# Key-value products of a linear-attention kernel: whole-array products over blocks of 128 successive tokens in place of products on quarters of the array

## Chip, cores and metric

The kernel runs on one core of a Trainium2 chip. The time is the device time of one execution in microseconds (us), median over the timed runs. Engines are named as in the profile: PE is TensorE's matmuls, PEld its weight loads, DVE VectorE, ACT ScalarE, POOL GpSimd, SP SyncE, which issues nearly all DMAs.

## What is computed

A Performer attention block is followed by a Fourier mixing block with an MLP. All tensors are f32; there are 8 batches, 8 heads, 576 tokens and 64 channels a head, and 128 random features.

```python
def phi(x):
    proj = np.einsum('bhsd,md->bhsm', x, omega)
    ...
    return np.exp(h) / np.sqrt(m)
q_p, k_p = (phi(q_s), phi(k_s))
kv = np.einsum('bhsm,bhsd->bhmd', k_p, v)
z = np.sum(k_p, axis=2)
num = np.einsum('bhsm,bhmd->bhsd', q_p, kv)
den = np.einsum('bhsm,bhm->bhs', q_p, z)[..., None] + 1e-06
return (num / den).astype(np.float32)
```

The result, with the heads side by side as 512 channels, is Fourier-transformed over tokens and channels; the real part is added to it, the sum is normalised, and an MLP with weights of 512 x 2048 and 2048 x 512 is added. The change concerns `kv` and `z` alone: a sum over the 576 tokens of a head, and so indifferent to the order in which they are taken.

## The kernel before

**Pairs.** The attention works on 32 pairs of heads, 4 to a batch. `loads` (L464) brings the keys of a pair into the first nine 64-channel columns of the tile `kq` and its queries into the next nine; there are two `kq` buffers. `load_v` (L476) brings the values into one of three tiles `vd`, whose 65th column holds ones, so that the product gives `kv` and `z` at once. All three use the same arrangement: partition `p` of 128 holds nine successive tokens, partitions 0 to 63 those of the first head and 64 to 127 those of the second.

**Steps of a pair** (`attn`, L668). Nine transposes of 128 x 128 (L607) turn `kq`; the scores (L701) multiply the turned tokens with `omega`, on half rows of the array for the first six pairs (`wide`) and on quarters for the others; `softmax` (L637) takes the maximum on DVE (L644) and the exponential on ACT (L661). The features of chunk `c` are then a 128 x 128 tile with tokens on the partitions. The key-value products (L732 to L741) take a 64 x 64 quarter of a feature tile as weights, 64 tokens of one head by half of its 128 features, and stream the 65 columns of `vd`. Nine chunks by two heads by two halves make 36 products in a pair, accumulated in PSUM as `kvp[feature, head, column]`, each head in a bank of its own. The step's copy to SBUF (L749 on DVE, L751 on ACT) follows. Query features are transposed (L607 again), and the numerators (L782, L790) use `kv` and are scaled into the token tile (L799 to L811).

**Beside it.** In the same stretch of time run the Fourier products of finished batches (L894, L904, L944, L955), the narrowing of the MLP weights (L532 to L550, loaded by SP at L564) and the first MLP products (L1236, L1259). The rest of the span is the MLP (L1727, L1878, L2178).

**Order.** Everything is cut into `Step`s, each with its engine, its cost as planned and its dependences. `Listing.run` (L272) orders them from written-down choices, one character a step (`PICKS`) and one a PSUM bank (`BANKS`). The choices fix the order of instructions on every engine; planned costs don't change it where a choice is written. An engine runs its instructions in that order and waits where a tile isn't there.

Of the kernel before, what the change touches and what calls it, by code (L numbers as in the profile page):

```python
# [375 lines left out]
def kernel(  # L376
# [10 lines left out]
    nc = tc.nc  # L387

    B, H, S, D = q.shape
# [13 lines left out]
    P = 128  # L403

    R = S // 64

    NS = 3
    NV = 3
# [38 lines left out]
        kq=NKQ, turned=NS, e=NE, e1=NS, kv=NS, x0=1, x1=1, fold=1, half=1, y=1,  # L447
# [8 lines left out]
    def got():  # L456

        return listing.got, psum_of(listing.got)
# [2 lines left out]
    kqs = {}  # L461
    vds = []

    def loads():  # L464
        for n in range(B * NP):
            b, pr = divmod(n, NP)
            h = slice(2 * pr, 2 * pr + 2)
            rows = "i (p r) d -> (i p) r d"
            yield Step(SP, 0.37, 3.0, take=("kq",), makes=("k", n), kb=288)
            kq = ld.tile([P, 2 * R, D], F32, name="kq", tag="kq")  # L470
            nc.sync.dma_start(kq[:, 0:R, :], k[b, h].rearrange(rows, r=R))
            kqs[n] = kq
            yield Step(SP, 0.47, 3.6, makes=("kq", n), kb=288, bias=-2.98)
            nc.sync.dma_start(kq[:, R : 2 * R, :], q[b, h].rearrange(rows, r=R))

    def load_v(n):  # L476
        b, pr = divmod(n, NP)
        yield Step(SP, 0.63, 4.0, take=(f"vd{n % NV}",), makes=("vd", n), kb=500, bias=0.52)
        nc.sync.dma_start(
            vds[n % NV][:, :, 0:D],  # L480
            v[b, 2 * pr : 2 * pr + 2].rearrange("i (p r) d -> (i p) r d", r=R),
        )

    def loads_v():
        for n in range(B * NP):
            yield from load_v(n)
# [181 lines left out]
    def attn(n):  # L668
        b, pr = divmod(n, NP)

        yield Step(NONE, after=(("k", n),) + ((("vd", n - 1),) if n else ()))
        kq = kqs.pop(n)
# [40 lines left out]
        def place(c):  # L713
            if c in (R - 1, R):
                return 2, c - (R - 1)
            return (c % 2, c // 2) if c < R else (3 + c % 2, (c - R - 1) // 2)

        def feature(c):
            t, i = place(c)
            return es[t][:, i, :]  # L720
# [8 lines left out]
            give=("e", "e", f"vd{n % NV}"), bias=-0.19,  # L729
        )  # L730
        kvb, kvp = got()
        for r in range(R):  # L732
            for i, h in ((0, 0), (1, 1), (0, 1), (1, 0)):
                rows, cols = slice(D * i, D * i + D), slice(D * h, D * h + D)
                nc.tensor.matmul(  # L735
                    kvp[cols, i, 0 : D + 1],
                    lhsT=feature(r)[rows, cols],
                    rhs=vds[n % NV][rows, r, :],
                    start=(r == 0),
                    stop=(r == R - 1),  # L740
                )  # L741
        kvs = []

        def keep():
# [32 lines left out]
        for i in range(2):  # L777
            for c in range(4):
                half = int(c in (1, 2))
                for g in range(2):  # L780
# [3 lines left out]
                        lhsT=flat[:, c0 : c0 + D],  # L784
                        rhs=kvs[0][:, i, :],
                    )

        for i in range(2):
            for g in range(2):
                nc.tensor.matmul(  # L790
                    ndp[D * g : D * g + D, i, (D + 1) * 4 : (D + 1) * 5],
                    lhsT=qeT[:, 0, D * i : D * i + D],
                    rhs=kvs[0][:, i, :],
# [775 lines left out]
    def pairs(start):  # L1569
        for n in range(start, B * NP, NS):  # L1570
            yield from attn(n)
# [45 lines left out]
    def betweens(text):  # L1617
# [6 lines left out]
    listing = Listing(buffers)  # L1624
    listing.run(
        [first(), loads(), loads_v(), load_tables(), frames(), plain_norms(), mixing()]
        + [pairs(i) for i in range(NS)]
        + [w2_parts(), weight_sums(), block_norms(0, mlpp), plain(), weights(), warm()],
# [766 lines left out]
```

## Time and profile before

| | |
|---|---|
| timed runs | 1120.97 us median of 3 (1120.73 to 1124.49) |
| profiled execution, span from first to last instruction | 1119.2 us |
| TensorE clock granted | 0.999 of full speed, on average |
| DMA | 196549 packets, 236.13 MB, 53808 of them under 512 B |
| DVE's maxima (L644) | 89.3 us in all |
| ACT's exponentials (L661) | 165.7 us in all |

The profile has no time of the profiled execution other than its span. A row of a group of instructions has its line, engine and operation, the tiles written and read, the part of the array (`64*64` is a quarter, `128*128` the whole), the size, the count, then busy time in us and the mean of one in ns. An f32 product is recorded as two passes, a transpose as one. Passes of different parts of the array may overlap, and the recorded duration of one holds a fixed tail, so distances between starts say more than durations. A row of the timeline has start, length, engine, line and count; instructions of one kind that follow each other are merged into one row. A row of the chain has start, length and what was being done.

### The profile page before, as it was taken

What the parts mean: (1) busy time and instruction counts of PE and PEld (TensorE: products, weight loads), DVE (VectorE), ACT (ScalarE), POOL (GpSimd) and SP (SyncE); (2) the same over time, 40 slices, a digit from 0 to 9 for tenths busy, and PEclk for the clock granted to TensorE, in tenths of its full rate; (3) what the DMA queues carried; (4) which work ended last, traced back from release to release, by engine and by line L of the source; (5) the groups of instructions that cost most, each with busy time, mean ns of one, the idle gap of its engine ahead of it and who ended that gap; (6) DMA issues with size and microseconds to landing.
All of it is one profiled execution on the core that took longest, in us unless ns stands there. A gap on an engine that the chain in (4) does not pass through costs nothing.

```text
span 1119.2 us, 31666 instructions
## 1 busy us (share of the span) xinstructions
PE 1108.4 (99%) x12467; PEld 1000.4 (89%) x12467; DVE 888.7 (79%) x1685; ACT 539.5 (48%) x1644; POOL 390.6 (35%) x401
## 2 busy tenths in 40 slices
PE   9999999999999999999999999999999999999998
PEld 7888888879868778999999889999889999889998
DVE  6999999987576767687697777888677888568895
ACT  7998898856536455623214452223463223331221
POOL 2443443553563348634413464000365000152000
PEclk9999999999999999999999999999999999999999
DMA  8856766665674669798896778747678656546453
GB/s 243 243 174 188 242 180 191 183 208 176 216 232 156 194 172 343 224 314 262 260 326 224 226 216 248 207 148 238 206 207 261 207 155 216 170 152 220 146 160 105
DMA packets 196549, 236.13 MB, mean 211 GB/s; under 512 B 53808, under 2 KB 120624, under 8 KB 196400
## 3 DMA queue, kind: packets, MB, share of 16 engines
q1 hardware_dynamic: 195904, 233.83, 68.1%
q8 instruction: 99, 1.62, 0.6%
q14 instruction: 50, 0.41, 0.1%
q10 hardware_dynamic: 496, 0.26, 0.1%
HBM read 182.13 MB, written 56.10 MB: 213 GB/s over the span
## 4 chain that ended last, share of the span: by engine, by line
PE 92%; DVE 3%; ACT 2%; DMA 2%; issue 0%; POOL 0%; SPq 0%; DVEq 0%; ACTq 0%
PE banks L2178 31%; PE banks L1727 27%; PE banks L1236 5%; PE banks L701 5%; PE banks L607 5%; PE banks L1259 5%; PE banks L1878 4%; PE banks L735 3%; PE banks L782 2%; PE banks L944 2%; PE banks L894 1%; ACT e L661 1%; DVE nmx L644 1%; PE banks L904 1%; DMA unw<-turned 1%; DMA raw<-in_moe_w_ch_dram 1%
## 5 line engine op out<-in xcount | busy, mean ns | idle before, releaser
L2178 PE MATMUL banks<-wl,sums 128*128 128x128 f32 x1792 | 219.8, 275 | 0.0
L2178 PEld LDWEIGHTS banks<-wl,sums 128*128 128x128 f32 x1792 | 210.6, 192 | 1.0 <-issue 0.3
L661 ACT ACTIVATE e<-banks,nmx 128x128 f32<-128x128 f32 x576 | 165.7, 441 | 23.3 <-DVE nmx L644 22.9
L644 DVE TENSOR_REDUCE nmx<-banks 128x8 f32<-128x1024 f32 (+1 forms) x96 | 89.3, 951 | 16.8 <-PE banks L701 12.4
L2178 PE MATMUL banks<-wl,hid 128*128 128x128 f32 x768 | 99.2, 275 | 0.3 <-DVE part L2154 0.3
L2178 PEld LDWEIGHTS banks<-wl,hid 128*128 128x128 f32 x768 | 92.8, 192 | 1.2 <-DVE part L2154 0.8
L2149 ACT ACTIVATE s<-banks 128x128 f32<-128x128 f32 x112 | 30.9, 277 | 113.6 <-PE banks L2178 103.5
L1727 PE MATMUL banks<-unw,wxw 128*128 128x256 f32 x352 | 85.4, 379 | 0.0
L701 PE MATMUL banks<-om,kqT 64*64 64x128 f32 (+1 forms) x2088 | 79.0, 275 | 1.7 <-ACT kv L751 1.3
L701 PEld LDWEIGHTS banks<-om,kqT 64*64 64x64 f32 (+1 forms) x2088 | 64.5, 138 | 12.7 <-issue 3.2
L2178 PE MATMUL banks<-wl,hx 128*128 128x128 f32 x576 | 74.2, 275 | 0.4 <-DVE part L2154 0.4
L1727 PEld LDWEIGHTS banks<-unw,wxw 128*128 128x128 f32 x352 | 66.6, 190 | 8.9
L1727 PE MATMUL banks<-rx,wxw 128*128 128x256 f32 x288 | 70.8, 379 | 0.0
L2178 PEld LDWEIGHTS banks<-wl,hx 128*128 128x128 f32 x576 | 69.4, 192 | 0.8 <-DVE part L2154 0.6
L1752 ACT ACTIVATE s<-banks 128x512 f32<-128x512 f32 x65 | 38.5, 596 | 65.1 <-PE banks L1727 60.0
L1727 PE MATMUL banks<-ttw,wxw 128*128 128x256 f32 x288 | 69.8, 379 | 0.0
L1236 PE MATMUL banks<-unT,w 128*128 128x128 f32 x512 | 65.4, 279 | 1.7 <-DVE qeT L621 1.7
L550 POOL TENSOR_TENSOR w<-w,raw 128x512 f32<-128x512 f32 x28 | 37.6, 1351 | 77.3 <-DVE raw L544 68.1
L2227 POOL TENSOR_TENSOR more<-more,part 128x512 f32<-128x512 f32 x2 | 2.6, 1315 | 176.6 <-ACT part L2220 176.6
L1236 PEld LDWEIGHTS banks<-unT,w 128*128 128x128 f32 x512 | 60.2, 192 | 4.5 <-issue 2.3
L1727 PEld LDWEIGHTS banks<-rx,wxw 128*128 128x128 f32 x288 | 54.5, 190 | 7.3
L1727 PEld LDWEIGHTS banks<-ttw,wxw 128*128 128x128 f32 x288 | 54.5, 190 | 7.3
(287 smaller groups left out, 2442.3 us busy)
## 6 DMA issues: line engine op xcount, KB each, us to landing
wl<-w2l SPq DMA_DIRECT2D x245, 256.0 KB, 3.9
wxw<-w1x SPq DMA_DIRECT2D x120, 256.0 KB, 3.1
raw<-in_moe_w_ch_dram SPq DMA_DIRECT2D x32, 512.0 KB, 4.8
kq<-in_k_dram SPq DMA_DIRECT2D x32, 288.0 KB, 4.5
kq<-in_q_dram SPq DMA_DIRECT2D x32, 288.0 KB, 4.5
vd<-in_v_dram SPq DMA_DIRECT2D x32, 288.0 KB, 5.4
ur<-us SPq DMA_DIRECT2D x30, 256.0 KB, 5.2
w2l<-sums SPq DMA_DIRECT2D x14, 512.0 KB, 4.9
```

The source lines that it names most:

```text
L550: eng.tensor_tensor(out=dst, in0=dst, in1=lof, op=ALU.add)
L607: nc.tensor.transpose(ps[:, (j - j0) * 128 : (j - j0 + 1) * 128], src(j), ident[:])
L644: nc.vector.tensor_reduce(nmx[:, :, 0:num], pps[:, :, 0 : MF * num].rearrange("p b (c m) -> p b c m", m=MF), axis=AX.X, op=ALU.max, negate ...
L661: nc.scalar.activation(out=e[:, c + (i if num == 1 else 0), :], in_=pps[:, i, MF * c : MF * c + MF], func=AF.Exp, bias=nmx[:, i, c : c + 1],)
L701: nc.tensor.matmul(pps[cols, c, MF * m : MF * m + MF], lhsT=kqT[rows, j, cols], rhs=om2[rows, :],)
L735: nc.tensor.matmul(kvp[cols, i, 0 : D + 1], lhsT=feature(r)[rows, cols], rhs=vds[n % NV][rows, r, :], start=(r == 0), stop=(r == R - 1),)
L1236: nc.tensor.matmul(hp[:, 0:TP], lhsT=w1[:, dc, 128 * fc : 128 * fc + 128], rhs=unTs[key][:, dc, :], start=(dc == 0), stop=(dc == NDC - 1),)
L1259: nc.tensor.matmul(yp[:, 0:DM], lhsT=hs[fc][:, 128 * i : 128 * i + 128], rhs=w2[:, fc, :], start=(fc == 0), stop=(fc == NFC - 1),)
L1727: nc.tensor.matmul(ps[:, span * f : span * f + span].rearrange("f (b q) -> f b q", q=Q), lhsT=left[:, P * f : P * f + P], rhs=right, start ...
L1752: nc.scalar.activation(out=s[:], in_=ps, func=AF.Copy)
L1878: nc.tensor.matmul(cell.rearrange("f t (b q) -> f t b q", q=Q), lhsT=w[:, d, col : col + 128], rhs=right[:, :, d].rearrange("f (t b) q -> ...
L2178: nc.tensor.matmul(ps[:, 0:128], lhsT=left[:, f], rhs=wls[head(j), i, n][:, f], start=start and f == 0, stop=(f == 3), skip_group_check=True,)
```

## The change

Keys and values are loaded another way. The two heads' 1152 tokens count as one list, and chunk `r` holds its tokens `128 r` to `128 r + 127`, one on each partition. Chunks 0 to 3 then belong to the first head alone and chunks 5 to 8 to the second; in chunk 4 the first 64 partitions are the first head's last tokens, the other 64 the second head's first. A key load that read 2304 successive bytes for each partition now reads nine pieces of 256 B; the value load read pieces of 256 B and still does. Queries are loaded as before.

Eight chunks are now one product each, with the whole 128 x 128 feature tile as weights; chunk 4 gives two, each with 64 tokens by 128 features. That makes 10 products in a pair. Step costs, choices, buffers and the order of steps are unchanged.

```diff
+    def across(src):
+        return src.rearrange("i s d -> (i s) d").rearrange("(r p) d -> p r d", r=R)
...
-            nc.sync.dma_start(kq[:, 0:R, :], k[b, h].rearrange(rows, r=R))
+            nc.sync.dma_start(kq[:, 0:R, :], across(k[b, h]))
...
-            v[b, 2 * pr : 2 * pr + 2].rearrange("i (p r) d -> (i p) r d", r=R),
+            across(v[b, 2 * pr : 2 * pr + 2]),
...
-        for r in range(R):
-            for i, h in ((0, 0), (1, 1), (0, 1), (1, 0)):
-                rows, cols = slice(D * i, D * i + D), slice(D * h, D * h + D)
-                nc.tensor.matmul(
-                    kvp[cols, i, 0 : D + 1],
-                    lhsT=feature(r)[rows, cols],
-                    rhs=vds[n % NV][rows, r, :],
-                    start=(r == 0),
-                    stop=(r == R - 1),
-                )
+        mid = R // 2
+        for r, i, rows in (
+            [(r, 0, slice(0, P)) for r in range(mid)]
+            + [(mid, i, slice(D * i, D * i + D)) for i in range(2)]
+            + [(r, 1, slice(0, P)) for r in range(mid + 1, R)]
+        ):
+            nc.tensor.matmul(
+                kvp[:, i, 0 : D + 1],
+                lhsT=feature(r)[rows, :],
+                rhs=vds[n % NV][rows, r, :],
+                start=(r == mid * i),
+                stop=(r == mid + mid * i),
+            )
```

## The prediction

> **What bounds the kernel now.** I read the page first: engine totals, then the chain of work that ended last.
>
> ```profile
> PE 1108.4 (99%) x12467; PEld 1000.4 (89%) x12467; DVE 888.7 (79%) x1685; ACT 539.5 (48%) x1644; POOL 390.6 (35%) x401
> PE 92%; DVE 3%; ACT 2%; DMA 2%; issue 0%; POOL 0%; SPq 0%; DVEq 0%; ACTq 0%
> ```
>
> TensorE is busy nearly always, and the chain runs through it for 92% of the span. But these are averages over stages, so next the windows, split where the attention work thins out and where it ends, and then the changed line itself.
>
> ```profile
> 0.00:160.00 160.00, 155.22 (x3365) 133.30 (x3366) 144.46 (x301) 139.53 (x504) 64.71 (x67) 1.00 0.71 209
> 160.00:360.00 200.00, 198.29 (x3719) 166.86 (x3718) 160.97 (x357) 129.87 (x461) 97.81 (x97) 1.00 0.64 199
> 360.00:1119.00 759.00, 754.86 (x5386) 700.21 (x5384) 583.25 (x1030) 270.10 (x682) 228.11 (x237) 1.00 0.70 215
> L735 PE MATMUL banks<-vd,e x2304: 213/218/268, 10.4 to 354.8; 64*64 64x65 f32 x192
> L735 PE MATMUL banks<-vd,e 64*64 64x65 f32 x2304 | 41.5, 219 | 0.2 <-issue 0.2
> ```
>
> Columns of the windows: the stretch, then PE, PEld, DVE, ACT and POOL busy, granted clock, DMA share, GB/s. All key-value products lie between 10.4 and 354.8 us. There are 36 x 32 = 1152 of them and 2304 records: an f32 product runs as two passes. In the first 160 us VectorE (144 of 160) and ScalarE (140) are nearly as full as TensorE; from 160 us on TensorE hardly idles. After 360 us nothing is touched, and a delay made before it is simply carried to the end. So the question is what the 32 blocks of L735 cost TensorE, and how much of that the first 160 us can swallow. For this I read the chain of the first 360 us in order of time:
>
> ```profile
> 10.47 1.46 PE banks L735 x72
> ...
> 352.90 2.10 PE banks L735 x144
> ```
>
> These are the first and the last of its 25 pieces in L735, 26 of the 32 blocks (the last piece holds two). The six blocks that it leaves out all lie before 100 us, where the chain goes through softmax on ScalarE and VectorE: the first and the last of them in the timeline are
>
> ```profile
> 15.92 1.08 PE L735 MATMUL banks<-vd,e 64*64 64x65 f32 x28
> ...
> 89.71 1.23 PE L735 MATMUL banks<-vd,e 64*64 64x65 f32 x72
> ```
>
> **The change, part by part.** *What one block costs now.* The timeline around one block:
>
> ```profile
> 149.67 0.57 PE L894 MATMUL banks<-cs_sb,fold 128*128 128x160 f32 x3
> 149.94 0.30 PE L894 MATMUL banks<-cs_sb,fold 128*128 128x160 f32 x1
> 150.17 0.54 PE L904 MATMUL banks<-cs_sb,fold 64*128 64x320 f32 x2
> 150.55 0.43 PE L904 MATMUL banks<-cs_sb,fold 64*128 64x320 f32 x2
> 150.91 1.28 PE L735 MATMUL banks<-vd,e 64*64 64x65 f32 x72
> 152.12 0.33 PE L607 MATMUL banks<-ident,e 128*128 128x128 f32 x1
> 152.29 0.30 PE L894 MATMUL banks<-sn_sb,fold 128*128 128x160 f32 x1
> ```
>
> Times are starts; a duration has a fixed tail, so I work from start to start. L894: (149.94 - 149.67)/2 = 0.135 us for a pass of 160 columns, 0.83 ns a column; 65 columns stream in 0.055. Where the array's division changes (full to halves at 150.17, halves to quarters at 150.91) more goes by: 0.23 instead of 0.135, and 0.36 instead of 0.27 for 320 columns. That is a **drain** of 0.09, and the first weight load after it is exposed too. The block: 152.12 - 150.91 = 1.21 = first load 0.055 + 18 sets of four passes + drain 0.095, so 0.059 a set: four quarters load and stream side by side. Beside quarter products (scores of pair 6 and later) drain and load go away:
>
> ```profile
> 252.01 0.40 PE L701 MATMUL banks<-om,kqT 64*64 64x128 f32 x8
> 252.23 1.23 PE L735 MATMUL banks<-vd,e 64*64 64x65 f32 x72
> 253.28 0.39 PE L701 MATMUL banks<-om,kqT 64*64 64x128 f32 x6
> ```
>
> 1.05 there, 18 x 0.0585.
>
> *What the new block costs.* Eighteen slots of 65 columns remain: 8 products x 2 passes on the whole array, and the two half products side by side, 2 passes. Streaming is no shorter. What grows is the weight load, 128 columns a pass where it was 64:
>
> ```profile
> 183.75 0.19 PEld L944 LDWEIGHTS banks<-sd_sb,y 128*128 128x128 f32 x1
> 183.86 0.30 PEld L944 LDWEIGHTS banks<-sd_sb,y 128*128 128x128 f32 x2
> 150.17 0.19 PEld L904 LDWEIGHTS banks<-cs_sb,fold 64*128 64x128 f32 x2 [0.17 <-issue]
> 150.17 0.30 PEld L904 LDWEIGHTS banks<-cs_sb,fold 64*128 64x128 f32 x4 [0.17 <-issue]
> L735 PEld LDWEIGHTS banks<-vd,e x2304: 129/135/137, 10.4 to 354.7; 64*64 64x64 f32 x192
> L2178 PEld LDWEIGHTS banks<-wl,sums 128*128 128x128 f32 x1792 | 210.6, 192 | 1.0 <-issue 0.3
> ```
>
> The first load after a drain at 183.75 keeps the second out until 183.86: 0.11. The mean durations agree: 192 against 135 ns, 57 ns for 64 more columns, so 128 take about 0.11 and 64 about 0.055. Nowhere in the trace do loads of 128 columns in one place start closer than 0.108. With 128 columns streaming (0.107) such a load is hidden; with 65 (0.055) it is not. A pass therefore costs **0.11, paced by the load**, against 0.059 for a set of four quarters. Inside a block:
>
> - four whole products, 8 passes: 7 x 0.11 + 0.055 = 0.825
> - whole to halves: drain 0.09 + load 0.11 = 0.20
> - the two half products: 0.11 + 0.06 = 0.17
> - halves to whole: 0.20
> - four whole products: 0.825
>
> 2.22 us, where the 18 sets took 1.06. The drains on either side change too: none beside whole-array work now, but one (0.20 in, 0.09 + 0.055 out) beside quarters. From the end of the stream before to the start of the next:
>
> - whole on both sides (6 blocks): 0.09 + 0.055 + 1.06 + 0.15 = 1.36 -> 2.22, +0.87
> - another division before, whole behind (7): 1.36 -> 2.42, +1.07
> - quarters before and whole behind (7), or the first score form on both sides (2): 1.21 -> 2.42, and 1.41 -> 2.62; +1.21
> - whole before, quarters behind (3): 1.21 -> 2.37, +1.16
> - quarters on both sides (5): 1.06 -> 2.57, +1.51
> - the last two, back to back: +2.42
>
> Sum: 5.22 + 7.49 + 10.89 + 3.48 + 7.55 + 2.42 = **37 us** of TensorE time. The six blocks off the chain are 3 x 0.87 + 1.21 + 2 x 1.51 = 6.8 of it; the 26 on it 30.2. What is on the chain is paid, since nothing else on it gets shorter. Of the 6.8, TensorE's waits in that stretch hide part; between none and all I take a third showing, 2, because softmax still ends last there and its engines' work is unchanged.
>
> *The keys' load.* Each partition had one run of 2304 B; now nine of 256 B, as the values have already.
>
> ```profile
> kq<-in_k_dram SPq DMA_DIRECT2D x32, 288.0 KB, 4.5
> kq<-in_q_dram SPq DMA_DIRECT2D x32, 288.0 KB, 4.5
> vd<-in_v_dram SPq DMA_DIRECT2D x32, 288.0 KB, 5.4
> L471 SPq DMA_DIRECT2D kq<-in_k_dram x32: 327/358/2035, 0.7 to 311.9; - x32
> L479 SPq DMA_DIRECT2D vd<-in_v_dram x32: 545/586/1519, 2.6 to 325.0; - x32
> PEld banks L607 <- DMA kq<-in_q_dram: 0.4, 2, 0.2
> ```
>
> By the values' rows a load lands 0.9 later at most and SP issues 0.23 longer. It is covered by the second kq buffer: in all, TensorE waited 0.4 us for kq. Uncovered once, ahead of the first pair: 0.5 to 0.9. Bounds over all: nothing, and 32 x 0.9 = 29 if each load were late; I take 1, by the 0.4 row. The values' load keeps its 256 B pieces, only in another order: nothing. Kept as they are: order, buffers, the copy of kv, every wait's source; a longer block delays only kv and numerators, and these are in the chain. SP's later loads (raw among them) wait for buffers that TensorE now frees later, which harms nothing while TensorE is the late one.
>
> Sum: 30.2 + 2 + 1 = +33 on a span of 1119.2, so 1152.4; the median of the runs is 1.8 above that span (what lies around it, and scatter): **1154**.
>
> A rule speaks for the change: the Trainium skill, TensorEngine Tiling (Array Packing), section Instruction Overhead, says that each matmul carries about 60 cycles, so that few columns cost as much as sixty. The rows above disagree: 72 passes take 1.05, 14.6 ns each. What this mechanism would give is rival 2.
>
> **Rivals.**
>
> 1. *The load doesn't pace the passes*: the next weights are loaded two ahead. Then a pass costs 0.059: 2.22 falls by 15 x 0.051 = 0.77, 25 over 32 blocks; +8 to +12, **1131**. For: loads and passes do overlap in the trace. Against: the 0.11 between the two loads of L944, and of L904. Chance 5%. A weaker form: a pass streams before its own load has ended, which spares the two exposed loads in each new block, 2 x 0.11 x 32 = 7 us, **1147**. Against it stands the first pass after a drain, 0.38 us where its form's later ones take 0.275, longer by just such a load:
>
> ```profile
> 183.75 0.38 PE L944 MATMUL banks<-sd_sb,y 128*128 128x129 f32 x1
> L944 PE MATMUL banks<-sd_sb,y x96: 270/275/378, 61.9 to 400.4; 128*128 128x129 f32 x32, 128*128 128x128 f32 x32, 128*64 128x129 f32 x16, 128*64 128x128 f32 x16
> ```
>
> Chance 3%. (The Trainium skill, TensorE: Matmul & The Clock Gate, section Architectural detail, says that a matmul can begin before its weight load is complete; these rows don't show it.)
> 2. *The array is paced by instructions* (faster): 14.6 ns a pass, so 20 passes where 72 were take 0.29 instead of 1.05, 0.76 x 32 = 24 less, **1097**. It decides if a pass's cost doesn't grow with its columns. Against: L701's sets of four at 128 columns take (252.23 - 252.01)/2 = 0.11, L735's at 65 0.0585. Chance 2%.
> 3. *Nothing is seen*: the waits swallow it all and VectorE's 144 of 160 us sets the end: **1121**. Against: TensorE's recorded idle time up to 360 us is 4.8 + 1.7, and 26 blocks are on the chain. Chance 2%. A softer form, where part of the 30 is hidden too because the chain hops between engines of nearly equal load: 1138 to 1147, chance 12%.
> 4. *More than the sum*: late key loads, or the two half products one behind the other (0.06 + 0.11 more a block, 5 us), or VectorE, idle while it waits for kv, late afterwards: 1161 to 1170, chance 9%.
>
> **How the numbers follow.** Forecast (1147 to 1161): 67%; rivals as above. The range, 1140 to 1163, leaves out rivals 1 to 3, part of the softer form, and the far end of 4: under 2 in 10. A measurement of this kernel tells about 0.5% (5.6 us) from no change. Slower: 96%; within: 2% (rival 3); faster: 2% (rival 2).
>
> **What would show it.** In the changed profile L735 has 320 products, 640 passes: 512 of form 128*128 and 128 of 64*128. Loads inside a block start 0.11 apart, and about 0.20 more is lost around the middle pair twice. A block takes 2.2 to 2.4 from first to next. The line's busy time, 41.5 now, goes to about 75 us, and the stage before 360 us ends about 33 later with an unchanged length behind it. Loads 0.06 apart would bring rival 1; blocks as long as said, but the stage's end under 25 later, the softer form of 3; TensorE waiting for kq by microseconds, rival 4.

## The result: 2.8% slower, 1153.6 us

The changed kernel takes 1153.62 us (median of 4 runs, 1152.58 to 1154.77) where the kernel before, measured beside it, takes 1121.49 (median of 4, 1120.73 to 1124.49). The medians lie 32.1 us apart. The ratio of the runs' means is 1.0281, 95% interval 1.0261 to 1.0301: of 1121.49 that is 31.5 us (29.3 to 33.8), against the +33 and the 1154 forecast. Differences below are worked out in this second way, from a ratio and the median of the kernel before that was measured beside it.

The profile's page of the changed kernel, with the rows that answer to those of before; first the engine totals and the chain's shares:

```profile
PE 1142.5 (99%) x10803; PEld 1032.3 (90%) x10803; DVE 891.2 (77%) x1685; ACT 541.0 (47%) x1644; POOL 388.3 (34%) x401
PE 95%; DVE 2%; DMA 1%; ACT 1%; issue 0%; SPq 0%; DVEq 0%; ACTq 0%
```

TensorE has 34.1 us more to do (1142.5 - 1108.4) with 1664 passes fewer (10803 for 12467); VectorE and ScalarE have the same work (2.5 and 1.5 us apart). The chain lies on TensorE for 95% where it was 92%. Then the stages, with the columns of the first such table; the last two stretches are cut where the old ones would lie if the attention's end had moved by 32 us:

```profile
0.00:160.00 160.00, 156.50 (x2326) 137.04 (x2329) 134.43 (x278) 129.79 (x463) 59.19 (x64) 1.00 0.73 198
160.00:360.00 200.00, 199.28 (x2663) 164.95 (x2656) 152.52 (x332) 125.25 (x443) 89.73 (x93) 1.00 0.64 180
360.00:392.00 32.00, 32.00 (x442) 30.11 (x442) 17.87 (x47) 16.02 (x60) 11.00 (x9) 1.00 0.48 170
392.00:1151.00 759.00, 754.70 (x5386) 700.18 (x5384) 586.39 (x1029) 269.94 (x682) 228.43 (x237) 1.00 0.70 215
```

The last stretch holds 5386 passes and 754.70 us, where the last 759 us of before held 5386 and 754.86. So all of the difference was made ahead of it, and then carried. In the first 160 us VectorE fell from 144.46 to 134.43 us of work and ScalarE from 139.53 to 129.79: they didn't get faster, they got less to do in that time, because TensorE is now the late one. The page's row of softmax's maxima says so, before and after (the number behind the second bar is the idle time ahead of them, then who ended it and how much of it):

```profile
L644 DVE TENSOR_REDUCE nmx<-banks 128x8 f32<-128x1024 f32 (+1 forms) x96 | 89.3, 951 | 16.8 <-PE banks L701 12.4
```

```profile
L648 DVE TENSOR_REDUCE nmx<-banks 128x8 f32<-128x1024 f32 (+1 forms) x96 | 89.5, 952 | 31.4 <-PE banks L705 25.0
```

VectorE waited 12.4 us for the scores and now waits 25.0. The changed line, in the views of groups, and then the timeline around a block between quarter products:

```profile
L742 PE MATMUL banks<-vd,e 128*128 128x65 f32 x512 | 69.6, 279 | 0.0
L742 PEld LDWEIGHTS banks<-vd,e 128*128 128x128 f32 x512 | 62.0, 191 | 6.5 <-issue 2.8 <-DVE qeT L625 0.3 <-ACT kqT L627 0.2
L742 PE MATMUL banks<-vd,e 128*128 128x65 f32 (+1 forms) x640 | 79.2, 283 | 0.0
```

```profile
234.87 0.62 PE L705 MATMUL banks<-om,kqT 64*64 64x128 f32 x16
235.42 2.51 PE L742 MATMUL banks<-vd,e 128*128 128x65 f32 x20
237.86 0.34 PE L705 MATMUL banks<-om,kqT 64*64 64x128 f32 x4
```

A load takes 191 ns where it took 135, and the block takes 237.86 - 235.42 = 2.44 us to the next product where a block between quarter products took 1.05. Beside whole-array work it is shorter, without the drain behind it:

```profile
224.47 2.41 PE L742 MATMUL banks<-vd,e 128*128 128x65 f32 x20
226.71 0.33 PE L1243 MATMUL banks<-unT,w 128*128 128x128 f32 x1
```

2.24. The weight loads of the block at 235.42, one row each for the first load and the first two, then for the middle pair, the first load of the second half, and the last two:

```profile
235.41 0.19 PEld L742 LDWEIGHTS banks<-vd,e 128*128 128x128 f32 x1 [0.17 <-issue]
235.41 0.30 PEld L742 LDWEIGHTS banks<-vd,e 128*128 128x128 f32 x2 [0.17 <-issue]
...
236.45 0.19 PEld L742 LDWEIGHTS banks<-vd,e 64*128 64x128 f32 x2
236.45 0.30 PEld L742 LDWEIGHTS banks<-vd,e 64*128 64x128 f32 x4
236.82 0.19 PEld L742 LDWEIGHTS banks<-vd,e 128*128 128x128 f32 x1
237.49 0.30 PEld L742 LDWEIGHTS banks<-vd,e 128*128 128x128 f32 x2
237.86 0.13 PEld L705 LDWEIGHTS banks<-om,kqT 64*64 64x64 f32 x1
```

A second load ends 0.11 after the first (0.30 for 0.19): the pace of the block. Seven such distances lead from 236.82 to the eighth load at 237.60 (the last two together, from 237.49, take 0.30), and then 0.26 pass to the next load of another division: 0.11 for that load itself, 0.055 for the last stream, and a drain of 0.09. From the middle pair's first load to the first of the second half 0.37 pass (236.82 - 236.45), which is 0.17 for the pair and 0.20 for the change back.

### The profile page after: what moved, and what is told of

It reads as the page before. It is cut to its first block, busy times and chain, and to the rows that moved or that the text cites. A ratio compares the mean times of both kernels' runs of the same rounds, so it can differ in the third digit from the quotient of the medians.

```text
span 1151.0 us, 28338 instructions
## 1 busy us (share of the span) xinstructions
PE 1142.5 (99%) x10803; PEld 1032.3 (90%) x10803; DVE 891.2 (77%) x1685; ACT 541.0 (47%) x1644; POOL 388.3 (34%) x401
## 4 chain that ended last, share of the span: by engine, by line
PE 95%; DVE 2%; DMA 1%; ACT 1%; issue 0%; SPq 0%; DVEq 0%; ACTq 0%
PE banks L2185 30%; PE banks L1734 26%; PE banks L742 6%; PE banks L705 6%; PE banks L611 5%; PE banks L1243 5%; PE banks L1266 4%; PE banks L1885 4%; PE banks L789 2%; PE banks L951 2%; PE banks L901 1%; PE banks L911 1%; PE banks L962 1%; PE banks L797 1%; DVE nmx L648 1%; DMA wl<-w2l 0%
## 5 line engine op out<-in xcount | busy, mean ns | idle before, releaser
L648 DVE TENSOR_REDUCE nmx<-banks 128x8 f32<-128x1024 f32 (+1 forms) x96 | 89.5, 952 | 31.4 <-PE banks L705 25.0
L742 PEld LDWEIGHTS banks<-vd,e 128*128 128x128 f32 (+1 forms) x640 | 71.6, 190 | 8.7 <-issue 2.8
L742 PE MATMUL banks<-vd,e 128*128 128x65 f32 (+1 forms) x640 | 79.2, 283 | 0.0
```

Of the source, the lines that this page charges most:

```text
L648: nc.vector.tensor_reduce(nmx[:, :, 0:num], pps[:, :, 0 : MF * num].rearrange("p b (c m) -> p b c m", m=MF), axis=AX.X, op=ALU.max, negate ...
L742: nc.tensor.matmul(kvp[:, i, 0 : D + 1], lhsT=feature(r)[rows, :], rhs=vds[n % NV][rows, r, :], start=(r == mid * i), stop=(r == mid + mid ...
```

## The experiments

The theory to be tested: the time went into the products, whose passes are paced by loads of 128 columns at 0.11 us, with two changes of the array's division in each block. The rivals: the loads of keys and values; the division alone; the depth of 128 rows or the stream. Times are compared with runs of the kernel before on the same chip at the same time, whose median was 1122.6 to 1123.7 there.

**Loads alone, products alone.** The quarter products with both new loads:

```diff
-            nc.sync.dma_start(kq[:, 0:R, :], k[b, h].rearrange(rows, r=R))
+            nc.sync.dma_start(kq[:, 0:R, :], across(k[b, h]))
...
-            v[b, 2 * pr : 2 * pr + 2].rearrange("i (p r) d -> (i p) r d", r=R),
+            across(v[b, 2 * pr : 2 * pr + 2]),
```

> Only the loads of keys and values are changed; the 36 quarter products are those of before, so kv mixes the two heads' tokens. Theory (the time went into the products' weight loads, which are twice as wide): 0 to +1 us on before, 1121 to 1123. Rival (the keys' smaller pieces land late or crowd the queue): +3 to +10, 1124 to 1132. By my sum the loads are 1 of the 33.

Measured: 1.0017 (1.0004 to 1.0029), +1.9 us. That lies between the two: above the theory's 0 to +1, below the rival's +3, with an interval (0.4 to 3.3) that reaches into both. The complement, the changed products on the loads of before:

```diff
-        for r in range(R):
-            for i, h in ((0, 0), (1, 1), (0, 1), (1, 0)):
...
+        for r, i, rows in (
...
+                lhsT=feature(r)[rows, :],
```

> Only the products are changed; keys and values are loaded as before, so kv mixes the two heads' tokens. Theory: all of the difference, 1152 to 1154. Rival (loads take part): under 1150. Together with the run of the loads alone it must add up to the 32 us measured.

Measured: 1152.77 us, 1.0263 (1.0248 to 1.0279), +29.5. The two add up to 31.4, the whole change to 31.5: 15 parts in 16 are the products'.

**Which load.** One of the two diffs above at a time.

> Only the keys' load is changed, values and products as before, so the features meet other tokens' values. Theory (the smaller pieces of the keys are what the loads cost): +1.5 to +2.5, like both loads together. Rival: 0 to +0.5.

Measured: 1.0022 (1.0010 to 1.0033), +2.5.

> Only the values' load is changed, keys and products as before, so the features meet other tokens' values. Theory: 0 to -1, since SP issues it in 0.43 us where it took 0.59 and it lands in 4.7 where it took 5.4. Rival (it is the values that cost): +1.5 to +2.5.

Measured: 1.0004 (0.9992 to 1.0016), +0.4 and not to be told from nothing. The two runs were measured side by side; their means lie 2.4 us apart (0.9 to 3.8). So it is the keys' pieces of 256 B that cost. The issue of the queries on SP before (shortest, median and longest in ns), then, of the run with the keys' load alone, the DMA rows, the same issue and TensorE's waits, and last the issue in the changed kernel:

```profile
L474 SPq DMA_DIRECT2D kq<-in_q_dram x32: 421/432/1784, 1.2 to 312.3; - x32
```

```profile
kq<-in_k_dram SPq DMA_DIRECT2D x32, 288.0 KB, 4.6
kq<-in_q_dram SPq DMA_DIRECT2D x32, 288.0 KB, 5.2
vd<-in_v_dram SPq DMA_DIRECT2D x32, 288.0 KB, 5.5
L478 SPq DMA_DIRECT2D kq<-in_q_dram x32: 415/894/2498, 1.2 to 317.2; - x32
PE banks L611 <- DMA kq<-in_q_dram: 1.9, 1, 1.9
PE banks L611 <- DMA kq<-in_k_dram: 0.9, 2, 0.5
```

```profile
L478 SPq DMA_DIRECT2D kq<-in_q_dram x32: 416/608/2739, 1.2 to 340.3; - x32
```

With the products of before, the keys' median landing hardly moves (4.6 for 4.5). The load *behind* them pays more: SP needs 0.89 us to issue the queries where it needed 0.43, they land at 5.2 where it was 4.5, and TensorE waited for them once, 1.9 us. Over all, TensorE's idle time (of products and weight loads) for the tile `kq`, from keys and queries, rose from 0.4 us before to 3.0 with the new keys' load, 2.3 with both loads and 0.7 with the values' load: +2.6, +1.9 and +0.3, where +2.5, +1.9 and +0.4 were measured. Each is one profiled execution, so the match may be in part luck.

With the new products it looks otherwise. Beside the run with the products alone the changed kernel's keys land later in the median (4.5 for 3.7) and so do its queries (4.7 for 4.3), whose issue takes 0.61 for 0.43; but TensorE's idle time for `kq` is 1.0 us there and was 1.2 with the products alone.

**The middle chunk on the whole array.** It removes both changes of division inside a block and adds two passes; the middle chunk's tokens count in both heads.

```diff
-            + [(mid, i, slice(D * i, D * i + D)) for i in range(2)]
+            + [(mid, i, slice(0, P)) for i in range(2)]
```

> The changed kernel with the middle chunk's two products on the whole array too, so chunk 4's tokens count in both heads: 20 passes of 128 x 128, and no change of the array's division inside a block. Theory: two slots more for the middle (4 x 0.11 where two slots and two drains with an exposed load took 0.17 + 2 x 0.20), 0.44 for 0.57, but the last stream of each part no longer ends in a drain: within 0 to -4 us of the changed kernel, 1149 to 1154. Rival (changing the division inside a block costs nothing): two passes more, +0.22 a block, 7 us, 1160.

Measured: 1152.43 us, 1.0260 (1.0242 to 1.0278), +29.2: 2.3 below the whole change's +31.5, within both intervals. Its blocks between quarter products:

```profile
234.61 2.45 PE L742 MATMUL banks<-vd,e 128*128 128x65 f32 x20
236.98 0.45 PE L705 MATMUL banks<-om,kqT 64*64 64x128 f32 x8
```

2.37 where 2.44 were. Twenty passes without a change of division are no dearer than eighteen slots with two: the rival, by which the changes are free, wanted 0.22 more a block and 1160 in all.

**Half the columns of a load.** Each whole product becomes two over 64 features, side by side; the streaming is the same, and there are 20 products in a block.

```diff
+            for g in range(2):
+                cols = slice(D * g, D * g + D)
...
-                kvp[:, i, 0 : D + 1],
-                lhsT=feature(r)[rows, :],
+                    kvp[cols, i, 0 : D + 1],
+                    lhsT=feature(r)[rows, cols],
```

> The changed kernel with each whole product cut into two over 64 of the 128 features: 128 rows by 64 columns, two side by side, and quarters in the middle chunk; 20 products in a block, the same streaming. A weight load is 64 columns again. Theory (the load paces): a set takes 0.059 and not 0.11, the block 0.465 + 0.145 + 0.117 + 0.145 + 0.465 = 1.34 for 2.22, 28 us less, and 2 to 4 us back for drains beside whole-array work: 1126 to 1131. Rival (a pass over 128 rows is dear whatever its columns, or the drains inside the block are what costs): above 1140.

Measured: 1131.40 us, 1.0076 (1.0059 to 1.0093), +8.5: 0.4 above the upper edge of what was expected, and 23 us less than the changed kernel. It computes the same from the same loads, so the 128 rows aren't what costs; the width of the load is.

```profile
L744 PEld LDWEIGHTS banks<-vd,e 128*64 128x64 f32 x1024 | 35.0, 137 | 7.8 <-issue 3.4 <-ACT kqT L627 0.8 <-ACT e L665 0.3
L744 PE MATMUL banks<-vd,e 128*64 128x65 f32 x1024 | 43.7, 227 | 0.0
L744 PE MATMUL banks<-vd,e 64*64 64x65 f32 x256 | 11.1, 243 | 0.0
212.30 1.58 PE L744 MATMUL banks<-vd,e 128*64 128x65 f32 x40
213.81 0.38 PE L1245 MATMUL banks<-unT,w 128*128 128x128 f32 x1
```

1024 loads of 137 ns are busy for 35 us where 512 of 191 ns were for 62. The last two rows give 1.51 us for a block where the changed kernel takes 2.24 to 2.44. The run keeps two changes of division in each block and adds one on each side wherever quarters stood beside quarters; that these make up all of the 8.5 us left is an inference, not a run of its own.

**Twice the stream.** Each product streams 128 columns, the 65 and others beside them that nobody reads.

```diff
-                rhs=vds[n % NV][rows, r, :],
+                rhs=flat[rows, c : c + P],
```

> The changed kernel, each product streaming 128 columns where it was 65 (the columns beside the 65 are other chunks' values, their sums are not read); the result is the reference's. Theory (the weight load of 0.11 paces, so a stream of 0.107 hides under it): only the stream's end ahead of each drain shows, 0.05 two or three times a block, 3 to 5 us: 1156 to 1160. Rival (streaming or rows pace): +0.05 to +0.10 a pass, 30 to 58 us, 1183 to 1212.

Measured: 1159.46 us, 1.0325 (1.0310 to 1.0339), +36.5, and so 5 us above the changed kernel.

```profile
239.61 2.67 PE L744 MATMUL banks<-vd,e 128*128 128x128 f32 x20
242.20 0.45 PE L705 MATMUL banks<-om,kqT 64*64 64x128 f32 x8
```

2.59 for 2.44, and 0.15 is what three stream ends of 0.05 ahead of a drain would give. The other fifteen slots took twice the columns for nothing. Together with the run before it this shows directly what paces a pass: halving the load's columns takes most of the cost away, doubling the stream's adds nothing to a pass.

**Which blocks show.** New loads and products for some pairs only, first the six that the chain of before leaves out, then the 26 others:

```diff
+        if n in (1, 4, 5, 7, 8, 9):
+            mid = R // 2
...
+        else:
+            for r in range(R):
+                for i, h in ((0, 0), (1, 1), (0, 1), (1, 0)):
```

> New loads and new products for the pairs 1, 4, 5, 7, 8 and 9 alone, whose blocks the chain of before leaves out; the others as before; the result is the reference's. Their added TensorE time is 6.8 us by my sum. Forecast: a third shows, +2, 1123 to 1125. Rival a (all of it shows, the chain says nothing on slack): +6 to +7, 1128. Rival b (all hidden): 1121 to 1122.

Measured: 1.0055 (1.0043 to 1.0068), +6.2. That is rival a.

> The counterpart: new loads and products for the 26 pairs on the chain, the six others as before; the result is the reference's. Forecast: +30, 1150 to 1152.5. Rival (the chain hops between engines of nearly equal load, part of the 30 is hidden too): under 1148.

Measured: 1.0269 (1.0254 to 1.0284), +30.2, as forecast. But 6.2 + 30.2 = 36.4 is more than the whole. Two more steps, the six pairs' products on the old loads, and the 26 again beside the whole change:

> New products for the pairs 1, 4, 5, 7, 8 and 9 alone and all loads as before, so kv of these six mixes the two heads' tokens. The six pairs with their loads gave +6. Theory a (the new loads took part in that, the blocks themselves have slack as the chain of before said): +2 to +4 on before. Theory b (the blocks off the chain show nearly whole when they alone grow): +5.5 to +7.

Measured: 1.0056 (1.0034 to 1.0077), +6.3: theory b, not the loads.

> The 26 pairs on the chain once more, beside the whole change on the same chip. Theory (the six blocks have slack once the others have grown, though not alone): within 2 us of the whole change, +30 on before. Rival (the six add their 6 wherever they stand, and the earlier difference of the two was scatter between chips): 5 to 7 below the whole change, +25 to +27.

> The changed kernel itself, beside the one with 26 pairs. Theory and rival: +31 to +33 on before; what counts is the distance to the other run.

Measured: the 26 pairs 1.0282 (1.0262 to 1.0301), +31.7; the whole change 1.0277 (1.0263 to 1.0291), +31.1. The rival is out: the six don't add their 6 wherever they stand. What they add on top of the 26 is known less well. Here the whole change is 0.6 us *below* the 26, with some 2.7 us either way by the two intervals; the first run of the 26, on another chip than the whole change, was 1.3 below it. Nothing and the 2 us of the forecast both fit. In the stretch from 40 to 100 us, where five of the six lie, first the two runs with 26, then the one with all 32:

```profile
40.00:100.00 60.00, 56.03 (x1182) 47.24 (x1184) 53.33 (x114) 53.18 (x198) 20.52 (x21) 1.00 0.66 187
```

```profile
40.00:100.00 60.00, 54.86 (x1159) 46.28 (x1159) 52.11 (x111) 52.34 (x195) 19.78 (x21) 1.00 0.66 185
```

```profile
40.00:100.00 60.00, 58.58 (x887) 50.09 (x885) 51.54 (x110) 51.46 (x192) 18.91 (x19) 1.00 0.67 181
```

With six blocks of the old size TensorE idles 4.0 and 5.1 us there, with the new 1.4; VectorE and ScalarE do nearly the same in all three. Where that idle time comes from is seen in part. The chains of both runs with 26 go through a load of queries at the same place, which the whole change's chain doesn't have; the later run's goes through a load of keys too, at 299.91, long behind the six blocks:

```profile
81.72 5.74 DMA kq<-in_q_dram
```

```profile
81.95 6.11 DMA kq<-in_q_dram
299.91 4.66 DMA kq<-in_k_dram
```

The later run's profiled execution is also the slowest of its four (1157.25 for a median of 1155.2). That the wait at 82 us makes the difference isn't shown, and stays open.

## Why the prediction was right, point by point

- **TensorE bounds the stage: right.** Its share of the chain rose from 92 to 95%, and TensorE's 34.1 us more of busy time went with 31.8 us more of span (1151.0 - 1119.2).
- **A pass is paced by its load, 0.11 us: right.** 0.11 in the rows of the block, and shown from both sides by the column halves and the doubled stream. The Trainium skill, TensorE: Matmul & The Clock Gate, section LDWEIGHTS, states the same as a rule: a load's time goes with its columns and not with its rows. These runs agree: 128 rows by 64 columns 137 ns, 64 rows by 64 columns 135, 128 by 128 191. One sentence of the working was too wide: that nowhere in the trace loads of 128 columns start closer than 0.108. It holds from product to product. Behind the load of a transpose, which is one pass, the next transpose's load starts 0.06 later in some fifty places of the kernel before (4.71 and 4.77, for one), and in the changed kernel a transpose's load starts 0.06 behind the last load of a block in 14. Why a transpose differs no run here shows; the price of a product's pass rests on the products' rows and the two runs, and stands.
- **Two changes of division in a block, 0.20 each: right.** The loads around the middle pair show 0.26 (with the last stream's 0.055) and 0.37 (with the pair's 0.17); without the two changes a block is 0.07 shorter, though it has two passes more.
- **A block's time: right.** 2.24 and 2.44 from its start to the next product, where 2.22, and 2.22 + 0.20 (the load ahead, the drain behind), were reckoned. The line's busy time came to 79.2 us, where about 75 was said: a block's recorded length, 2.41 or 2.51, holds the tail of its last pass too.
- **The keys' load, 1 us: right in part, and too small for the load alone.** The step was that keys land up to 0.9 later, by the values' row. With the products of before they don't in the median (4.6 for 4.5), and what the step leaves out, the issue and the landing of the queries behind them, grows; with the new products they do (4.5 for 3.7). Alone the keys' load costs 2.5 (1.1 to 3.7), with the values' 1.9 (0.4 to 3.3). The part that lies bare at the start was right: the first load of keys lands 3.8 us after its issue where it was 3.0, as the first transposes show, before and after:

```profile
3.84 0.81 PE L607 MATMUL banks<-ident,kq 128*128 128x128 f32 x4
```

```profile
4.64 0.52 PE L611 MATMUL banks<-ident,kq 128*128 128x128 f32 x3 [0.68 <-DMA kq<-in_k_dram]
```

  They begin 0.8 later, and 0.68 of it TensorE sat idle for the keys.
- **The six blocks off the chain, 2 of 6.8: not contradicted for the whole change** (-0.6 and +1.3 by the two comparisons, each with some 2.7 either way), **wrong as a statement on those blocks**: alone they show 6.2. The step took the chain for a measure of slack. A chain says which work ended last at each step, not by how much: on what lies beside it, it gives no slack.
- **The rivals: fell.** The block's loads 0.11 apart leave no room for rival 1, nor do its 2.44 us for the weaker form; the 1153.6 us lie far from rival 3 and above its softer form; and TensorE's 1.0 us of waiting for `kq` is not the lateness of rival 4. As for rival 2 (paced by instructions), the column halves' block of 40 passes beats the changed one's of 20, by 23 us in all. Read as a cost of each product, the rule in the Trainium skill, TensorEngine Tiling (Array Packing), section Instruction Overhead, would have had it the other way. The same page's Key Properties state that a change of tiling mode drains the engine, which the 0.26 above bears out; the larger part of a block's growth is the pace of its loads.
- **The layout of the sum: right in total, in part by luck.** For the products 30.2 + 2 = 32.2 was forecast, and alone they cost 29.5 (27.9 to 31.3); for the loads 1, and alone they cost 1.9. So less of the blocks' 37 us showed than forecast and the loads cost more, and the two errors partly cancel. The total of 33 is 1.5 above the measured 31.5, within its interval. The term for what lies around the span, 1.8, is what the profiled execution shows (1152.8 - 1151.0); the median of the runs lies 0.8 above that execution.

## What to carry to other kernels

Fewer and larger products are not fewer cycles: with f32 and few streamed columns, price a pass by the larger of its weight columns and its streamed columns (here 0.11 us with 128 weight columns and 65 or 128 streamed, 0.135 with 160 streamed), and see whether smaller tiles load side by side. Count what changes the array's division, for each cost a drain of 0.09 and a bare load here. And don't read slack off the chain: for what lies beside it, measure.

## What the runs showed of the hardware

Loads of 128 weight columns paced f32 products at 0.11 us a pass, whether 65 or 128 columns were streamed; cut into two loads of 64 columns side by side, over the same 128 rows, a block fell from between 2.24 and 2.44 us to 1.51.

A DMA in many small pieces delays the one behind it on the same queue: with nine pieces of 256 B a partition in the keys' load, the queries' load behind it was issued in 0.89 us (alone) or 0.61 (in the changed kernel) where it was 0.43. How much later the keys themselves landed differed from run to run: 3.8 us for 3.0 in the first load, 4.6 for 4.5 in the median beside the old products, 4.5 for 3.7 beside the new.

The values' load, whose pieces are 256 B in both arrangements, is issued faster when successive partitions read successive tokens: the changed kernel's row, against 545/586/1519 before,

```profile
L483 SPq DMA_DIRECT2D vd<-in_v_dram x32: 368/429/1926, 3.6 to 353.1; - x32
```

It is 0.43 with the values' load alone too, but there it lands no sooner (5.5 for 5.4) and makes no difference to the time.
